# A bank table by block and group for the partial sums, and the written order of a block laid out anew

## The chip, the cores and the metric

The kernel runs on one core of one Trainium2 chip. TensorE (PE) multiplies, VectorE (DVE), ScalarE (ACT) and GpSimd (POOL) work beside it, SyncE (SP) issues transfers, and each engine takes its instructions in the order in which they are written. PSUM, where PE adds up its products, has eight banks of 128 partitions x 512 f32 values. The metric is the device time of one run in microseconds.

## The reference

Eight sequences of 4096 tokens with 192 channels go through a causal convolution with seven taps per head, softmaxed over the taps, and then through a feed-forward layer with SiLU, all in f32:

```
w = exp(weight - max); w = w / (sum(w) + 1e-09)              # 8 heads x 7 taps
out[b,s,h,:] = sum_k w[h,k] * x_pad[b, s+k, h, :]            # 24 channels a head
h = out @ w_in                                               # 192 -> 2048
g = h * (1.0 / (1.0 + np.exp(-h)))
result = g @ w_out                                           # 2048 -> 192
```

There are 32768 tokens, `w_in` is 192 x 2048 and `w_out` 2048 x 192.

## The kernel before

**Tiling.** The tokens are cut into NB = 32 blocks of 1024 (two halves of 512). Block 0 is multiplied plainly (lines 571 and 762) while the weights are rounded and combined. From block 1 on, both layers use a scheme with fewer multiplications: operands are first added and subtracted, and the products are combined by further sums.

**First layer, form R (64 rows x 128 columns of PE).** The 2048 hidden columns form five groups g = 0 to 4 and one plain chunk. A group has fifteen products `P0.g` to `P14.g` (`product`, line 611, matmul at line 625). Each has 64 rows of depth, so it sits on row group 0 or 1 (the lower or upper 64 rows). Row group 1 has r = 0, 1, 2, 4, 5, 6, 11, 14, and group 0 the others; P14.4 sits on group 0. An f32 matmul is two passes in the profile, each with its own weight load. The products of a group add up in three chains:

```
CHAINS = ((5, 2, 6, 1, 0, 14), (3, 9, 7, 4, 8), (12, 10))
```

P13 and P11 go on top of the mid-chain sums X2 and X4. After single products the chain is read while it is still open: `u` (ACT, line 674) copies the first chain to one of ten tiles in SBUF ("u tiles", handed round in a list); `X` and `a` (DVE, line 668) add the second chain to such a copy, into a bank (X) or SBUF (a); `b` (DVE) subtracts the third chain; `S` (ACT, line 686) applies SiLU. The next product of the chain waits until the reader is through with the bank, and a new chain waits for the last reader of what stood in its bank before. The plain chunk is `L.nk` (line 642; `L.0k` on group 0 alone at full width, `L.1k` on both groups at half width), with `SL` for its SiLU.

**Second layer, form C (128 rows x 32 columns).** `D i.je` (`out_slot`, line 711, matmul at line 741) is four matmuls side by side in the columns. They add into accumulator i of the block; `D5` is a quarter as wide. `t` (DVE, line 709) makes differences of the hidden values for them; `x`, `y`, `z` (ACT) and `M` (DVE) combine the accumulators, `o` transposes and `st` stores (SP).

**The next block's input.** `ld` loads (SP), `i` transposes (DVE), `ha` brings the six tokens before the block, `v.ki` is tap i of channel third k: an ACT copy into a u tile and a DMA from POOL's queue that adds it to `nat` (lines 494 and 495; for blocks up to 3 on DVE). `sp` spreads the result into the slots of `dup` (SP), and `w` (DVE) makes the combined operands in `win`. `dup` and `win` exist once.

**Order.** `PLAN` is a list of such tokens and is run once for each b from 3 to 33. A token without a sign belongs to block b, `-` to b - 1, `=` to b - 2, `+` to b + 1. So the products of a block share an iteration with the second layer of the block before. `START` is a longer list of the same kind that is run once, with b = 2, and holds blocks 0 to 2; the last C work of block 31 is in `finish`. Every instruction is pinned to this order on its engine.

**Banks.** One table serves all blocks:

```
QUEUE = (0, 4, 1, 2, 3)
CHAIN_BANKS = ((0, 1, 7, 1, 0), (2, 3, 2, 3, 2), (4, 4, 4, 4, 4))
PLAIN_BANKS = (7, 4, 3)
ACC = (7, 1, 3, 5, 6, 4, 0)
XBANK = {2: 5, 4: 6}
```

`CHAIN_BANKS[c]` has the bank of chain c for the groups in the order of `QUEUE`, `ACC` that of each accumulator. The third chain is in bank 4 for every group.

The end of R in an iteration, and the point where two late products of group 0 and block b stand between D tokens:

```
-D5.00 -S5.2 -S1.2 v.01 v.02 -D3.10 -D3.11 -S5.3 -t.20 v.23 v.24 P5.0 -P8.3 v.12 -D1.30 ...
P0.3 u1.3 b5.2 a1.2 P7.3 P12.3 S0.1 S0.0 a5.3 b1.3 P8.2 +i.1 P11.3 P14.3 S2.3 S3.3 P4.3 P10.3 D0.21 D1.20 ...
```

Of the kernel before, what the change touches and what calls it, by code (L numbers as in the profile page):

```python
# [17 lines left out]
def kernel(  # L18
# [63 lines left out]
        "-S4.3 -D1.11 -sp.0 -S1.4 -D0.11 -S5.1 -D1.01 -D0.01 -a0.2 -D1.00 -D0.10 -t.01 -t.03 "  # L82
        "-D4.01 -D4.00 ha.0 v.10 -t.10 -t.11 -S5.4 -b5.3 -D2.00 v.20 v.21 -S0.2 -t.02 -D3.01 "
        "-D2.11 -a1.3 -sp.1 -D0.31 -D2.01 -D2.10 v.00 -D3.00 -t.13 -t.12 -D5.01 v.11 v.22 -S1.3 "
        "-D4.11 -D4.10 -D5.11 -D5.00 -S5.2 -S1.2 v.01 v.02 -D3.10 -D3.11 -S5.3 -t.20 v.23 v.24 "
        "P5.0 -P8.3 v.12 -D1.30 -t.21 -D2.20 -t.23 -D4.21 -D4.20 -D5.10 -D2.21 -D0.20 -sp.2 "
        "v.03 v.04 -D5.20 -t.22 -a0.3 -D3.21 -D1.10 -w.0 -S0.3 -t.30 -t.31 -t.32 v.13 -D2.31 "
        "-D1.31 -t.33 -D5.30 -D0.00 v.05 -w.1 -w.2 -w.3 -w.4 -w.5 -D0.30 -D1.21 -D5.31 -D5.21 "
        "-x2.1 v.14 -y1.0 -D4.30 -x2.0 u5.0 -D2.30 -y2.0 -z1.0 -D3.20 -M1.0 -D4.31 -x1.0 -x2.3 "
        "-x2.2 -y0.0 +ld.1 -M2.0 -D3.31 -D3.30 -M3.0 -M4.0 P2.0 +ld.0 u4.0 P3.0 L.02 P5.4 u5.4 "  # L90
        "-x0.0 L.00 P6.0 L.12 -M5.0 u2.0 L.01 X2.0 -M7.0 P2.4 u4.4 SL.0 L.10 L.11 P9.0 SL.1 "
        "X4.0 SL.2 P1.0 u0.0 P6.4 u2.4 -M6.0 P13.0 S2.0 P5.1 u5.1 -o.3 P3.4 P7.0 P0.0 u1.0 "
        "+ld.2 P12.0 P11.0 P1.4 X2.4 P9.4 a5.0 P4.0 P13.4 b1.0 v.25 S4.0 X4.4 P10.0 a1.0 b5.0 "
        "P2.1 u0.4 P0.4 P7.4 -o.1 S2.4 a5.4 P11.4 v.26 P8.0 a0.0 u4.1 u1.4 S1.0 S4.4 P12.4 P6.1 "
        "b1.4 u2.1 P14.4 P14.0 S3.4 P3.1 X2.1 P4.4 S3.0 a1.4 P5.2 u5.2 P10.4 b5.4 P9.1 P1.1 "
        "X4.1 u0.1 -o.2 P2.2 v.06 P8.4 a0.4 P5.3 u4.2 P7.1 -st.3 a5.1 P0.1 -o.0 u5.3 u1.1 S5.0 "
        "P12.1 b1.1 P6.2 u2.2 P3.2 P4.1 a1.1 P13.1 S2.1 X2.2 P2.3 u4.3 P10.1 v.15 P1.2 u0.2 "
        "P8.1 a0.1 -st.1 b5.1 P11.1 P13.2 S4.1 S2.2 P9.2 P6.3 P14.1 P3.3 P0.2 S1.1 +i.2 P12.2 "
        "X4.2 P7.2 P11.2 u2.3 P1.3 X2.3 S3.1 P9.3 u1.2 b1.2 S4.2 P10.2 u0.3 P14.2 S3.2 v.16 "
        "-st.2 a5.2 P4.2 P13.3 X4.3 P0.3 u1.3 b5.2 a1.2 P7.3 P12.3 S0.1 S0.0 a5.3 b1.3 P8.2 "  # L100
        "+i.1 P11.3 P14.3 S2.3 S3.3 P4.3 P10.3 D0.21 D1.20 t.00 S0.4 -st.0 +i.0"
    )
    START = (
        "=dp.28 =v.20 =v.10 =dp.44 =v.00 =dp.18 =dp.6 =dp.40 =dp.7 =dp.32 =dp.23 =dp.30 =dp.13 "
        "=dp.2 =dp.20 =dp.24 =dp.15 =dp.35 =dp.14 =dp.33 =dp.11 -ld.1 =dp.37 =dp.36 =dp.25 "
        "-ld.2 =dp.27 =dp.17 -ld.0 =dp.0 =v.11 =dp.34 =v.01 =dp.26 =v.12 =dp.29 =v.21 =v.13 "
        "=dp.45 =v.22 =dp.21 =v.02 =dp.42 =v.14 =v.03 =dp.39 =v.15 =dp.3 =v.04 =dp.38 =v.16 "
        "=dp.47 =v.23 =sp.1 =v.05 =dp.1 =v.24 =dp.22 -i.1 =dp.12 =v.25 =v.06 =dp.43 =v.26 =go.2 "
        "=sp.0 =dp.19 -i.0 =dp.46 -i.2 =dp.31 -ha.0 =dp.9 =sp.2 =dp.4 =dp.41 -v.10 -v.00 -v.11 "
        "=dp.8 -v.20 -v.01 =dp.5 -v.12 =dp.16 -v.02 =w.0 =dp.10 =w.1 =cp.0 -L.01 -P5.0 -v.03 "  # L110
        "=cp.1 -L.02 -P5.4 =w.2 -u5.0 -L.10 =w.3 -u5.4 -P2.0 -P3.0 -v.13 -P2.4 -u4.0 -v.04 "
        "-P6.0 -L.00 -u4.4 -L.12 -u2.0 -L.11 -SL.0 -X2.0 -P6.4 -SL.2 =w.4 =cp.2 -P9.0 -P1.0 "
        "-u2.4 =o.0 -P13.0 -P5.1 -v.14 -u0.0 -X4.0 -P3.4 -P1.4 -S2.0 =w.5 -SL.1 -P7.0 -P11.0 "
        "-u5.1 -X2.4 -u0.4 -P12.0 -P0.0 -a5.0 -v.21 -P13.4 -P0.4 -u1.0 =o.1 -P4.0 -P9.4 -u1.4 "
        "-v.15 -S4.0 -P2.1 -P14.4 -a1.0 -b1.0 -P14.0 -P8.0 -u4.1 -X4.4 -S3.4 -P6.1 -P10.0 -v.22 "
        "-S2.4 -a0.0 -P11.4 -P7.4 -u2.1 -b5.0 -S3.0 -P5.2 -P3.1 -S4.4 -a5.4 -P1.1 -P12.4 -u5.2 "
        "-X2.1 -P4.4 -u0.1 -P9.1 -b1.4 -P2.2 -a1.4 -P10.4 -X4.1 -P5.3 -u4.2 -P8.4 =o.2 -P6.2 "
        "-b5.4 -P13.1 -u5.3 =st.2 -a0.4 -P0.1 -P7.1 -u2.2 -v.23 -S2.1 ld.1 -P2.3 -P3.2 -a5.1 "
        "-u1.1 -S0.0 -P1.2 -P12.1 -X2.2 -S0.4 -P4.1 -u4.3 -P13.2 -b1.1 ld.2 -S1.4 -P6.3 -a1.1 "
        "-u0.2 -P10.1 -v.24 -P11.1 -u2.3 -P8.1 -b5.1 -P0.2 -S4.1 -P9.2 -v.05 -S2.2 -a0.1 -P12.2 "  # L120
        "-P1.3 -u1.2 -X4.2 -S0.1 -P3.3 -P14.1 -b1.2 -u0.3 -S5.4 -P7.2 -P11.2 -X2.3 -v.16 -P10.2 "
        "-P0.3 -S4.2 -a5.2 -sp.1 -P9.3 -P14.2 -u1.3 -b5.2 -S3.1 -P13.3 -P4.2 -X4.3 -S3.2 -S1.0 "
        "i.1 -P14.3 -P12.3 =st.0 -S1.1 -a1.2 -P11.3 -P7.3 -S5.0 -v.06 -S1.2 -t.00 -D0.00 =st.1 "
        "-S3.3 -S2.3 -D1.20 -b1.3 -S5.1 ld.0 -S4.3 -t.01 -D0.01 -S5.2 -D0.21 -t.02 -D1.11 -sp.0 "
        "-a5.3 -D1.10 -v.25 -t.03 -P8.2 P5.0 +ld.1 -P4.3 -P10.3 -D1.30 -b5.3 -v.26 -D1.00 -a0.2 "
        "-sp.2 -D4.01 -t.10 -S0.2 -D5.00 -D2.01 i.0 -D4.00 -t.11 -D2.00 i.2 -D5.01 ha.0 -t.13 "
        "-D0.11 -D3.00 -a1.3 +ld.2 -D3.01 -t.12 v.10 -D4.11 -w.0 v.00 +ld.0 -D5.10 v.11 v.20 "
        "-D5.11 -D2.10 u5.0 -t.20 -D0.20 -w.1 -D3.11 -t.21 -D4.10 -w.2 -D2.11 -t.23 -P8.3 P2.0 "
        "-D0.31 -a0.3 -t.22 -D3.10 -S0.3 -S1.3 -D4.21 v.21 -S5.3 u4.0 v.01 -D4.20 -t.30 -D3.20 "
        "-D5.21 -t.31 -D2.20 -D5.20 -D2.21 -D0.10 -t.32 -D2.30 v.02 -D1.01 -t.33 -D0.30 v.03 "  # L130
        "-D1.31 v.12 -D2.31 v.04 v.22 -D1.21 v.05 -D3.30 -y1.0 -w.3 -z1.0 -D5.30 v.13 -D5.31 "
        "-D3.31 -x2.0 -M1.0 -x2.1 -D4.31 -x2.2 v.14 -x2.3 -y2.0 -M2.0 -D3.21 -y0.0 v.06 -D4.30 "
        "-x0.0 -w.4 v.23 -x1.0 P3.0 P5.4 -M3.0 L.10 u5.4 -w.5 P6.0 L.02 -M4.0 L.11 u2.0 L.00 "
        "P2.4 X2.0 P1.0 L.01 -M5.0 u4.4 v.15 L.12 u0.0 P6.4 P9.0 SL.2 SL.0 P0.0 P13.0 X4.0 SL.1 "
        "u2.4 -M7.0 P3.4 P5.1 S2.0 +i.0 P7.0 P1.4 u5.1 X2.4 P12.0 P11.0 u0.4 a5.0 u1.0 v.24 "
        "P9.4 P2.1 S4.0 b1.0 P4.0 P13.4 u4.1 X4.4 P14.0 P10.0 a1.0 P0.4 P7.4 S3.0 b5.0 v.25 "
        "P11.4 P8.0 u1.4 a5.4 S2.4 P6.1 P12.4 a0.0 P14.4 P4.4 u2.1 b1.4 v.26 P5.3 P3.1 S3.4 "
        "a1.4 S4.4 P10.4 P1.1 X2.1 P5.2 P8.4 -M6.0 u0.1 b5.4 P9.1 P0.1 u5.2 -o.1 u5.3 P13.1 "
        "P2.2 X4.1 -st.1 u1.1 +i.2 P12.1 P2.3 u4.2 a0.4 S2.1 P7.1 P6.2 b1.1 u4.3 P3.2 a5.1 P6.3 "
        "u2.2 P10.1 S5.4 X2.2 P4.1 u2.3 S0.4 P9.2 b5.1 P1.2 S0.0 a1.1 P13.2 P11.1 S1.0 -o.0 "  # L140
        "u0.2 P8.1 v.16 P1.3 S2.2 S4.1 sp.1 P0.2 P12.2 a0.1 u0.3 X4.2 S5.0 P3.3 P14.1 u1.2 +i.1 "
        "P7.2 P11.2 X2.3 -st.0 b1.2 P9.3 P0.3 S4.2 a5.2 +ha.0 P10.2 u1.3 X4.3 P4.2 S0.1 P7.3 "
        "b5.2 P14.3 S1.1 a1.2 S3.1 P12.3 P14.2 S3.3 a5.3 P13.3 -o.3 P4.3 S3.2 b1.3 -st.3 +v.10 "
        "P8.2 +v.20 a1.3 P10.3 P11.3 S5.2 t.00 S2.3 -o.2 -st.2 D0.21 D1.20"
    )
    QUEUE = (0, 4, 1, 2, 3)
    CHAIN_BANKS = ((0, 1, 7, 1, 0), (2, 3, 2, 3, 2), (4, 4, 4, 4, 4))
    PLAIN_BANKS = (7, 4, 3)
# [453 lines left out]
    ACC = (7, 1, 3, 5, 6, 4, 0)  # L602
    XBANK = {2: 5, 4: 6}

    def chain_bank(g, c):
        return banks[CHAIN_BANKS[c][QUEUE.index(g)]]

# [3 lines left out]
    def product(b, g, r, half=None):  # L611
        cols = columns(half)
        e = int(r in ON_B and (g, r) != SWAP)
        if r in RIGHT:
            rhs = rows(wins[b], e)[:, RIGHT[r], :]
        else:
            rhs = rows(dups[b], e)[:, SLOT[e][X_OF[r]], :]
        if r in (13, 11):
            to, first = banks[XBANK[2 if r == 13 else 4]], False
        else:  # L620
            c = next(c for c in range(3) if r in CHAINS[c])
            to, first = chain_bank(g, c), r == CHAINS[c][0] and (b, g, c) not in begun
            begun.add((b, g, c))
        pin(
            nc.tensor.matmul(  # L625
                to[:, cols],
                raw(g, *LEFT[e][r], e),
                rhs[:, cols],
                start=first,
                stop=True,  # L630
                skip_group_check=True,
            )
        )

    def plain(b, n, k):
# [3 lines left out]
        for e in range(2) if n else (0,):  # L639
# [3 lines left out]
                    banks[PLAIN_BANKS[n and 1 + e]][:, cols],  # L643
# [67 lines left out]
    def out_slot(b, j, i, e, half=None):  # L711
# [7 lines left out]
        if at not in accs.setdefault(b, {}):  # L719
            accs[b][at] = banks[ACC[at]]  # L720

# [389 lines left out]
```

## Time and profile before

| | us |
|---|---|
| runs (three) | 2353.54, 2353.54, 2353.39 (median 2353.54) |
| profiled execution | 2352.7, span 2351.0, granted clock 1.00 |
| PE busy | 2343.4 (100% of the span) |
| DVE, ACT, POOL busy | 1802.6, 1507.6, 528.7 |
| block 0, plain: line 571, line 762 | 41.2, 41.35 in the chain |

From about 110 us on, the same pattern returns every 72.24 us. In such a stretch (863.51 to 935.75 us) PE is busy for 72.24, DVE for 54.62, ACT for 48.54 and POOL for 15.63 us, and the DMA engines for 0.63 of the time. PE is called busy whenever any matmul is in flight, so the row says nothing of how full its two row groups or four column groups are. That has to be read from the starts of single passes, in the timeline. Times of starts are from the span's start.

### The profile page before, as it was taken

What the parts mean: (1) busy time and instruction counts of PE and PEld (TensorE: products, weight loads), DVE (VectorE), ACT (ScalarE), POOL (GpSimd) and SP (SyncE); (2) the same over time, 40 slices, a digit from 0 to 9 for tenths busy, and PEclk for the clock granted to TensorE, in tenths of its full rate; (3) what the DMA queues carried; (4) which work ended last, traced back from release to release, by engine and by line L of the source; (5) the groups of instructions that cost most, each with busy time, mean ns of one, the idle gap of its engine ahead of it and who ended that gap; (6) DMA issues with size and microseconds to landing.
All of it is one profiled execution on the core that took longest, in us unless ns stands there. A gap on an engine that the chain in (4) does not pass through costs nothing.

```text
span 2351.0 us, 45656 instructions
## 1 busy us (share of the span) xinstructions
PE 2343.4 (100%) x17630; PEld 1123.6 (48%) x17630; DVE 1802.6 (77%) x2373; ACT 1507.6 (64%) x2779; POOL 528.7 (22%) x672
## 2 busy tenths in 40 slices
PE   9999999999999999999999999999999999999998
PEld 5344554445544455444555444554445544455544
DVE  8998777787777777777777778777777777777776
ACT  5346766667666676666776666766667666677643
POOL 4920222221222211222122222122221122212200
PEclk9999999999999999999999999999999999999999
DMA  7234566665566665666656666556666566755511
GB/s 158 52 66 79 96 101 117 117 111 101 97 113 113 116 108 91 113 110 120 104 100 100 117 117 112 103 95 114 113 113 108 99 108 111 123 102 101 85 33 21
DMA packets 523833, 238.81 MB, mean 102 GB/s; under 512 B 431648, under 2 KB 436768, under 8 KB 523616
## 3 DMA queue, kind: packets, MB, share of 16 engines
q0 software_dynamic: 73024, 133.73, 33.5%
q1 hardware_dynamic: 447392, 101.78, 24.5%
q8 instruction: 138, 2.26, 0.4%
q10 hardware_dynamic: 3200, 0.39, 0.1%
q14 instruction: 79, 0.65, 0.1%
HBM read 31.46 MB, written 25.17 MB: 24 GB/s over the span
## 4 chain that ended last, share of the span: by engine, by line
PE 100%; DVE 0%; ACT 0%; issue 0%; ACTq 0%; DVEq 0%
PE ps L741 48%; PE ps L625 44%; PE ps L642 3%; PE ps L762 2%; PE ps L571 2%; PE ps L1010 1%; PE ps L418 0%; DVE cmb L158 0%; ACT u L158 0%; DVE osb L158 0%; DVE xt L460 0%; PE ps L444 0%; ACTq L944 0%; DVE zeros L158 0%; DVE xt L158 0%
## 5 line engine op out<-in xcount | busy, mean ns | idle before, releaser
L495 POOL DMA_DIRECT2D nat<-u x504 | 431.5, 953 | 1606.5 <-ACT u L494 830.7
L625 PE MATMUL ps<-win,wr 64*128 64x512 f32 x1550 | 685.8, 598 | 0.0
L741 PE MATMUL ps<-g,wo 128*32 128x512 f32 x2976 | 681.4, 594 | 0.0
L625 PE MATMUL ps<-win,ws 64*128 64x512 f32 x1550 | 629.5, 596 | 0.0
L674 ACT COPY u<-ps 128x512 f32<-128x512 f32 x775 | 452.3, 584 | 133.3 <-PE ps L625 110.7
L741 PE MATMUL ps<-t,wo 128*32 128x512 f32 (+2 forms) x4528 | 523.6, 446 | 0.0
L741 PE MATMUL ps<-t,wx 128*32 128x512 f32 x2976 | 474.7, 592 | 0.0
L686 ACT ACTIVATE g<-g 128x512 f32<-128x512 f32 x465 | 277.2, 625 | 262.6 <-DVE g L668 262.6
L625 PE MATMUL ps<-dup,wr 64*128 64x512 f32 x868 | 420.2, 598 | 0.0
L709 DVE TENSOR_TENSOR t<-g,t 128x1024 f32<-128x1024 f32 x248 | 303.0, 1222 | 134.5 <-PE ps L741 125.7
L709 DVE TENSOR_TENSOR t<-g 128x1024 f32<-128x1024 f32 x248 | 301.6, 1216 | 65.4 <-PE ps L741 65.2
L668 DVE TENSOR_TENSOR g<-u,ps 128x512 f32<-128x512 f32 x465 | 313.7, 678 | 41.4 <-PE ps L625 38.6
L494 ACT ACTIVATE u<-xt,taps 128x512 f32<-128x512 f32 x504 | 340.1, 711 | 5.1 <-DMA nat<-u 2.9
L625 PEld LDWEIGHTS ps<-win,wr 64*128 64x128 f32 x1550 | 261.6, 187 | 113.4 <-issue 61.8
L668 DVE TENSOR_TENSOR ps<-u,ps 128x512 f32<-128x512 f32 x310 | 215.0, 693 | 131.2 <-ACT u L674 60.6
L625 PEld LDWEIGHTS ps<-win,ws 64*128 64x128 f32 x1550 | 254.6, 187 | 124.2 <-issue 53.5
L686 ACT ACTIVATE g<-ps 128x512 f32<-128x512 f32 x465 | 267.4, 597 | 57.0 <-PE ps L625 56.8
L625 PE MATMUL ps<-dup,ws 64*128 64x512 f32 x682 | 291.9, 599 | 0.0
L741 PEld LDWEIGHTS ps<-t,wo 128*32 128x32 f32 x4528 | 180.3, 110 | 221.6 <-issue 192.7
L741 PE MATMUL ps<-g,wx 128*32 128x512 f32 x1488 | 251.4, 594 | 0.0
L741 PEld LDWEIGHTS ps<-t,wx 128*32 128x32 f32 x2976 | 121.2, 110 | 241.0 <-issue 240.6
L741 PEld LDWEIGHTS ps<-g,wo 128*32 128x32 f32 x2976 | 167.6, 110 | 135.3 <-issue 125.9
(92 smaller groups left out, 1883.0 us busy)
## 6 DMA issues: line engine op xcount, KB each, us to landing
nat<-u POOLq DMA_DIRECT2D x504, 256.0 KB, 4.2
dup<-nat SPq DMA_DIRECT2D x345, 128.0 KB, 2.4
nat<-in_x_dram SPq DMA_DIRECT2D x382, 64.0 KB, 4.1
out_dram<-osb SPq DMA_DIRECT2D x376, 64.0 KB, 2.1
raw<-in_moe_w_out_dram SPq DMA_DIRECT2D x8, 384.0 KB, 3.6
raw<-in_moe_w_in_dram SPq DMA_DIRECT2D x12, 192.0 KB, 4.4
ws<-wr POOLq DMA_DIRECT2D x8, 192.0 KB, 4.7
raw<-in_moe_w_in_dram SPq DMA_DIRECT2D x6, 128.0 KB, 3.0
```

Source lines behind the costliest of these rows:

```text
L494: pin(nc.scalar.activation(z, src, AF.Copy, scale=tap))
L495: pin(nc.gpsimd.dma_start(out=dst, in_=z, accum_op=ALU.add))
L571: nc.tensor.matmul(hs[a, n, e], rows(wr[j], e)[:, a, k, :], rows(d, e)[:, n, k, :], start=k == 0, stop=k == NK - 1,)
L625: nc.tensor.matmul(to[:, cols], raw(g, *LEFT[e][r], e), rhs[:, cols], start=first, stop=True, skip_group_check=True,)
L642: nc.tensor.matmul(banks[PLAIN_BANKS[n and 1 + e]][:, cols], rows(wr[j] if own == e else ws[j], e)[:, a, k, :], rows(dups[b], e)[:, SLOT[e ...
L668: pin(nc.vector.tensor_tensor(out_, u, v, op=op))
L674: pin(nc.scalar.copy(us[b, g, o][:, cols], t1[:, cols]))
L686: pin(nc.scalar.activation(h, src, AF.Silu))
L709: pin(nc.vector.tensor_tensor(t[i // 2][:, i % 2, :], u, v, op=ALU.subtract))
L741: nc.tensor.matmul(accs[b][at][SQ * q : SQ * q + SQ, to], lhs[:, e, SQ * k : SQ * k + SQ], rhs[:, e, ts(q, TB // 4) if i == 5 else to], st ...
L762: nc.tensor.matmul(banks[DOWN_BANKS[k]][R * n : R * n + R, :], wo[j][:, a, e, R * k : R * k + R], gs[b, j, a][:, n, e, :], start=j == 0 an ...
L1010: nc.tensor.matmul(by_pe[k][n], rows(diag, n)[:, k, i, :], rows(xts[0], n)[:, k, i : i + TB], start=i == 0, stop=i == K - 1,)
```

## The change

Every table of banks gets one entry for each chain, mid-chain sum, plain sum and accumulator, by group, and three versions: for block 1, block 2, and all later ones. The lookups take the block. `PLAN` and `START` are written anew. They hold the same tokens apart from some signs. Nothing that is computed changes.

```diff
-    CHAIN_BANKS = ((0, 1, 7, 1, 0), (2, 3, 2, 3, 2), (4, 4, 4, 4, 4))
-    PLAIN_BANKS = (7, 4, 3)
+    CHAIN_BANKS = (
+        ((1, 0, 1, 3, 6), (5, 7, 5, 4, 2), (3, 6, 6, 1, 4)),
+        ((0, 0, 3, 7, 4), (3, 1, 6, 2, 6), (1, 2, 5, 1, 5)),
+        ((0, 7, 0, 6, 2), (4, 1, 3, 2, 5), (6, 4, 1, 5, 3)),
+    )
+    XBANKS = (
+        ((7, 3, 2, 2, 4), (7, 5, 0, 7, 4)),
+        ((5, 4, 4, 0, 5), (7, 5, 5, 4, 7)),
+        ((3, 4, 5, 4, 3), (1, 2, 5, 7, 6)),
+    )
+    PLAIN_BANKS = (
+        (0, 2, 3),
+        (2, 2, 1),
+        (6, 5, 7),
+    )
+    ACC = (
+        (3, 2, 5, 6, 7, 1, 0),
+        (4, 6, 3, 5, 1, 7, 0),
+        (4, 7, 5, 1, 3, 6, 0),
+    )
...
-    ACC = (7, 1, 3, 5, 6, 4, 0)
-    XBANK = {2: 5, 4: 6}
-
-    def chain_bank(g, c):
-        return banks[CHAIN_BANKS[c][QUEUE.index(g)]]
+
+    def of_block(table, b):
+        return table[min(b, len(table)) - 1]
+
+    def chain_bank(b, g, c):
+        return banks[of_block(CHAIN_BANKS, b)[c][g]]
+
+    def x_bank(b, g, o):
+        return banks[of_block(XBANKS, b)[o // 2 - 1][g]]
+
+    def plain_bank(b, i):
+        return banks[of_block(PLAIN_BANKS, b)[i]]
...
-            accs[b][at] = banks[ACC[at]]
+            accs[b][at] = banks[of_block(ACC, b)[at]]
...
-    DOWN_BANKS = (4, 5, 6)
+    DOWN_BANKS = (7, 4, 2)
```

The new `PLAN`, without the stretch of D tokens in its middle (where a line of dots stands for lines left out):

```
P5.0 -a1.3 -P10.2 -a0.2 -P10.3 -b5.3 -P8.3 -S4.3 -sp.0 -D0.31 -S0.1 -S1.0 -D1.10 v.20
-S3.3 -D1.30 -S1.4 -D1.21 -D0.00 -t.00 -t.01 -D2.00 -D2.01 =st.1 v.11 -t.03 -D4.01
-S1.1 -t.10 -D4.00 -D5.00 v.00 v.01 -D0.10 -sp.2 -t.11 -D2.10 -D1.01 v.12 -b5.2 v.02
...
-D3.01 -D1.11 -D5.11 -w.1 -D5.01 +ld.2 -D1.31 v.14 v.04 -D0.11 -D3.11 -D1.20 -a0.3
v.15 u5.0 -S1.2 -S0.2 -t.20 -D0.20 -t.21 -D2.21 -t.22 -S0.3 -D2.20 -w.2 v.22 -S1.3
+ld.1 -S5.3 -t.23 -D4.20 -D4.21 -D5.21 -D5.20 -D3.20 v.05 -t.30 -t.31 -D1.00 -t.33
-D2.31 -D5.31 -D5.30 -x2.2 -x2.0 v.23 -D0.30 -D0.21 -D0.01 -y0.0 v.06 -t.32 -z1.0 v.24
+ld.0 -D2.30 -w.3 -y1.0 -D3.21 -x2.3 -x2.1 -M1.0 -w.5 -D3.30 v.25 -D3.31 -x0.0 -D4.30
-D4.31 -y2.0 P2.0 -x1.0 -w.4 -M2.0 u4.0 -M6.0 P5.4 u5.4 P3.0 L.00 -M3.0 -M4.0 L.11
v.16 P6.0 -M5.0 -M7.0 L.02 u2.0 P2.4 u4.4 X2.0 v.26 L.12 -o.3 L.10 SL.1 SL.2 +i.0 P1.0
u0.0 L.01 SL.0 P6.4 u2.4 P13.0 -o.0 S2.0 -o.2 P9.0 P5.1 P3.4 X4.0 P0.0 u1.0 X2.4 P12.0
P11.0 P7.0 S4.0 b1.0 a5.0 P1.4 P14.0 -st.2 P13.4 u5.1 +i.2 P10.0 u0.4 S3.0 b5.0 P4.0
...
b1.4 P14.4 P11.4 P10.4 u2.1 a0.0 S3.4 S4.4 a5.4 P2.2 u4.2 P4.4 X2.1 P13.1 S2.1 b5.4
P9.1 a1.4 +i.1 P1.1 X4.1 P6.2 P3.2 u0.1 P8.4 a0.4 u2.2 X2.2 P5.3 P0.1 u5.3 P7.1 +ha.0
P11.1 S0.0 P12.1 P2.3 P9.2 a5.1 P4.1 P13.2 u1.1 b1.1 P10.1 P1.2 a1.1 +v.10 S4.1 u4.3
sp.1 S2.2 X4.2 b5.1 u0.2 P6.3 u2.3 P3.3 S5.1 X2.3 S0.4 P14.1 P8.1 a0.1 P11.2 S4.2 P7.2
P0.2 S3.1 a5.2 u1.2 P9.3 X4.3 P12.2 P1.3 P4.2 S5.0 a1.2 u0.3 b1.2 P13.3 S2.3 P7.3 a5.3
P14.2 S3.2 P0.3 u1.3 P12.3 S5.4 -st.0 P11.3 P8.2 b1.3 P4.3 P14.3
```

In `PLAN` the last line is followed by the first one of the next iteration.

## The prediction

> **What bounds the kernel now.** I read the page first, then the chain in order of time, then the timeline of TensorE (PE) and of its weight loads (PEld) at the places where the chain changes line.
>
> ```profile
> PE 2343.4 (100%) x17630; PEld 1123.6 (48%) x17630; DVE 1802.6 (77%) x2373; ACT 1507.6 (64%) x2779; POOL 528.7 (22%) x672
> PE 100%; DVE 0%; ACT 0%; issue 0%; ACTq 0%; DVEq 0%
> ```
>
> PE sets the end; no other engine holds a share of the chain. A gain or a loss is therefore time in which PE's row or column groups do nothing, and that does not show as idle PE. The chain of one block:
>
> ```profile
> 904.25 29.82 PE ps L625 x135
> 934.08 18.82 PE ps L741 x192
> 952.90 1.06 PE ps L625 x4
> 953.96 17.54 PE ps L741 x192
> 971.49 1.48 PE ps L625 x5
> ...
> 976.50 29.82 PE ps L625 x135
> ```
>
> The same line returns after 72.25 us. A block is a stretch of L625 and L642 (products, call it R) and L741 (D tokens, call it C), and it changes form four times: R, C 18.82, a detour of two products (P5.0, P8.3) of 1.06, C 17.54, R. Now the timeline at the detour:
>
> ```profile
> 879.61 1.04 PE L741 MATMUL ps<-t,wo 128*32 128x512 f32 x8
> 880.59 0.69 PE L625 MATMUL ps<-dup,wr 64*128 64x512 f32 x1
> 880.59 0.69 PE L625 MATMUL ps<-win,wr 64*128 64x512 f32 x1
> 881.12 0.59 PE L625 MATMUL ps<-dup,wr 64*128 64x512 f32 x1
> 881.12 0.59 PE L625 MATMUL ps<-win,wr 64*128 64x512 f32 x1
> 881.64 0.63 PE L741 MATMUL ps<-g,wx 128*32 128x512 f32 x3
> ```
>
> Each product is two passes. On one row group passes start 0.429 us apart, so a product takes 0.858 there, and the other group (other 64 rows) runs beside it. After a change of form the first pass takes 0.53 (its weights are not loaded ahead), and the last 0.52. A trip C to R and back costs 0.11 (last D token, 0.972 for 0.858) + 0.10 + 0.10 + 0.025 = 0.34 us. Last, the end of R, PE and then PEld:
>
> ```profile
> 930.47 0.59 PE L625 MATMUL ps<-win,ws 64*128 64x512 f32 x1
> 930.66 1.02 PE L625 MATMUL ps<-win,wr 64*128 64x512 f32 x2
> 931.10 0.69 PE L625 MATMUL ps<-dup,wr 64*128 64x512 f32 x1
> 931.52 0.59 PE L625 MATMUL ps<-win,wr 64*128 64x512 f32 x1
> 931.63 0.59 PE L625 MATMUL ps<-dup,wr 64*128 64x512 f32 x1
> 931.95 0.59 PE L625 MATMUL ps<-win,wr 64*128 64x512 f32 x1
> ```
> ```profile
> 930.66 0.19 PEld L625 LDWEIGHTS ps<-win,wr 64*128 64x128 f32 x1 [0.24 <-issue]
> 931.09 0.19 PEld L625 LDWEIGHTS ps<-win,wr 64*128 64x128 f32 x1 [0.24 <-issue]
> 931.09 0.29 PEld L625 LDWEIGHTS ps<-dup,wr 64*128 64x128 f32 x2
> 931.52 0.19 PEld L625 LDWEIGHTS ps<-win,wr 64*128 64x128 f32 x1
> ```
>
> The order there is P0.3 (row group 1), P7.3, P12.3, P8.2 (all 0), P11.3 (1). Group 1 is free at 930.47 + 0.43 = 930.90, but P11.3 (the dup,wr row) starts at 931.10, right after P12.3 has started and the weights of its second pass have been issued. It then runs ahead of P8.2 (931.95), which stands before it. So PE passes over waiting work of the other group, but not over any amount. I counted this over all PE and PEld rows, at the moment its own group came free: of 487 loads with five loads and passes of the other group waiting ahead of them, 280 left within 0.06 us (readers of banks held the rest); of 34 with seven to nine ahead (P11.3 in 30 blocks) none did, and the least late was 0.51 late. Call this the limit of five.
>
> **The parts.** A block holds 40 full D tokens at 0.858 and 8 D5 at 0.218: 36.07 us. On each row group it holds 39 products or L.0 and three half-width L.1 at 0.43: 34.76. Together 70.83, so 1.41 of the 72.24 is loss: two trips, 0.68, and waits inside R of 0.71 (0.27 round P10.4 and P9.1, where P9.1 waits for X2.1 to read bank 2 and for DVE, which restarts it unloaded; 0.44 from P7.3 to P10.3, where b1.3 reads bank 4, which all groups' third chain shares). The work itself is unchanged: the same 9,331 tokens, 17,144 matmuls, and on ACT, DVE, POOL and SP the same instructions in another order.
>
> *One trip less.* P5.0 and P8.3 join P10.2 and P10.3 at the end of R: -0.34.
>
> *Bank waits.* The third chain gets several banks, so P10.3 no longer waits last, and X2.1 reads well before P9.1. I went through the new order product by product, setting each reader (u 0.585, X 0.69, a 0.68, b 0.69; starts 0.60 apart when queued, 0.59 from a pass's start to its end, 0.04 to 0.05 each way between engines) against the row group's next product. The old -0.71 goes. One wait comes: a0.4, X2.2 and a5.1 stand in a row on DVE behind P8.4, and P4.1 needs a5.1. From P8.4's second pass this takes 0.59 + 0.04 + 0.60 + 0.61 + 0.68 + 0.05 = 2.57. Row group 1 has 3.00 until P4.1 if both groups run level, but group 0 is 0.51 late here (next part), leaving 2.49: a wait of 0.08 to 0.11 and a restart of 0.10. Bounds: 0 (level) and 0.6 (P9.2, P13.1, P6.2, P11.0, P4.0 have 0.16 to 0.24 to spare by the same reckoning; two of them late with a restart each). I take +0.22, nearest to the P9.1 stop.
>
> *The limit of five in the new order.* It stands at two places. P2.4, L.12, L.10, P1.0, L.01: L.01 must pass L.10 and P1.0 of group 1, so it waits 0.43 and starts unloaded: 0.51 late, but group 0 has that to spare. Then the end: P4.3, P14.3, P5.0 (all group 1), P10.2, P10.3, P8.3 (all group 0). P10.2 cannot pass until P14.3 has started; then it starts unloaded (0.11) and three products follow on group 0, 2.57, while group 1 has only P14.3 and P5.0 left, 1.72. R ends 0.97 later than level groups would. Bounds: 0 (no limit) and 2.15 (no passing). The P11.3 rows are the same situation: +0.97. This is the term that eats the gain.
>
> The Trainium skill, in TensorE: Matmul & The Clock Gate, section "Step-by-step: what each phase is for", says that only weight loads are pulled ahead and matmuls stay in program order. By that rule P10.2 would start with P5.0's second pass, 1.18 later than in my sum; the trace speaks against it, since P11.3 starts 0.85 before P8.2.
>
> *Moved conv steps.* v.11 to v.05 lie in C as before (12 pairs of an ACT copy, 0.71, and a POOL DMA, 4.2 to landing), v.23, v.06, v.24, v.25, v.16, v.26 now at the end of C and early in R, not spread over R. ACT has 48.5 busy of 72.2 and waits in C; cost 0 while the u tiles come free (rival below). *Moved on SP:* sp.1 and ha.0's two DMAs go to the end of R, the load order becomes 2, 1, 0, and st.1 goes one iteration later, behind sp.0, which waits for P13.3 and P14.3. Some 37 issues of about 0.55, 20 us of 72; sp.1 should land 4 us before P5.0. Cost 0. *START:* 153.3 us now; by the same prices 150.85, so 2.5 of waits. It has as many changes of form as before. Bounds -2.5 to +2.5; with the bank waits shorter I take -1.0. *End:* one trip less, -0.3.
>
> **Sum.** Per block -0.34 - 0.71 + 0.22 + 0.97 = +0.14; by stretches 36.07 + 34.76 + 0.34 + 0.97 + 0.22 = 72.36, +0.12. Times 29 blocks: +3.5; START and end -1.3: +2.2. The profiled execution took 2352.7 (span 2351.0), so 2354.9; the median of the runs stands 0.8 above it: 2355.7, say 2355. Within 0.2% (4.7 us) is about what a measurement can tell from no change.
>
> **Rivals.**
> - *The limit does not bind* (faster). Then both 0.97 and 0.22 go, -1.05 x 29 - 1.3 = -32: 2322. Against it: those 34 cases. The Trainium skill, TensorEngine Tiling (Array Packing), "Key Properties", has the tiles operate independently, which would give this; the 931.10 row disagrees. 0.11.
> - *The limit binds, R's other waits go, START gains more:* -0.11 x 29 and -4: about 2345. 0.14.
> - *Small DVE waits* (slower): two of the products with 0.16 to 0.24 to spare stop, 0.2 each: +11, 2366. For it: DVE is busy some 31 of R's 36 us. 0.22.
> - *The u tiles run out* (slower). u1.0 reuses the tile that v.25's DMA reads. v.23, v.24, v.25 follow one another on one nat slice; at 4.2 each, v.25 is in 2.2 before u1.0, and P14.0 has 0.9 more. It decides from about 5.2 each (landings of up to 6.8 occur); at 5.5 it is 0.8 a block, +23: 2377. Against it: single ones land in 3.3. 0.06.
> - *No passing at all:* +1.18 x 29 = +34: 2389. Refuted by the P11.3 rows, unless those are special. 0.03.
>
> **Numbers.** My forecast, no change, 0.44, with a range of its own of 2349 to 2358. Faster 0.11 + 0.14 = 0.25; slower 0.22 + 0.06 + 0.03 = 0.31. Leaving out 2322, 2377 and 2389 (0.20), the range is 2342 to 2370.
>
> **What would show it.** One R and one C piece per block in the chain, no 1.06 piece. At R's end a first weight load of P10.2 (dup,ws) right after P14.3's first pass, and R's end with only group 0 at work for about 0.9 us. L.01 about half a microsecond late. P9.1 and P10.3 without a wait on DVE, P4.1 with one. A period of 72.1 to 72.6. I am wrong if P10.2 starts beside P4.3 (period near 71.2), or if ACT waits for POOL at u1.0.

## The result and the profile after

| | before | after |
|---|---|---|
| median of the runs, us | 2353.54 | 2368.28 (2367.17 to 2368.87, four runs) |
| ratio | | 1.0062, 95% interval 1.0045 to 1.008 |
| profiled execution (span) | 2352.7 (2351.0) | 2367.17 (2365.1) |
| period of a block from block 4 on | 72.24 | 72.55 |
| START, first pass to first pass of the next iteration | 153.34 | 156.24 |

The changed kernel is 0.62% slower: 14.7 us by the medians, 14.5 between the profiled executions. The forecast was no change, 2355. Two stretches hold the loss. The blocks take 0.31 us more each, 29 times, 9.0 us. START takes 2.9 more although two products and two D tokens, 2.57 us of PE's work, have moved out of it to the last iterations: 5.5 in all, which is also what the blocks' 9.0 leave of the 14.5.

The page of the changed kernel, busy times and the chain's shares:

```profile
PE 2352.3 (99%) x17630; PEld 1156.1 (49%) x17630; DVE 1797.8 (76%) x2373; ACT 1503.1 (64%) x2779; POOL 530.3 (22%) x672
PE 97%; DVE 2%; issue 0%; SPq 0%; ACT 0%; DMA 0%; DVEq 0%; ACTq 0%
```

PE is idle for 12.8 us of the span (7.6 before), and DVE now holds 2% of the chain: that is START. The chain of one block, in order of time (start, length, what):

```profile
871.76 36.22 PE ps L765 x384
907.98 1.48 PE ps L649 x5
...
944.31 5.70 PE ps L765 x49
```

C (L765) is one piece and no 1.06 us piece of products stands in it: the second trip is gone. R now lasts from 907.98 to 944.31. Its end, PE and then PEld:

```profile
940.44 0.59 PE L649 MATMUL ps<-win,wr 64*128 64x512 f32 x1
...
941.46 1.13 PE L649 MATMUL ps<-dup,ws 64*128 64x512 f32 x4
942.32 0.59 PE L649 MATMUL ps<-dup,wr 64*128 64x512 f32 x1
...
942.75 0.59 PE L649 MATMUL ps<-dup,wr 64*128 64x512 f32 x1
...
943.29 1.02 PE L649 MATMUL ps<-win,wr 64*128 64x512 f32 x2
944.24 1.07 PE L765 MATMUL ps<-g,wo 128*32 128x512 f32 x8
```
```profile
941.46 0.30 PEld L649 LDWEIGHTS ps<-dup,ws 64*128 64x128 f32 x3 [0.24 <-issue]
```

P8.2 (win,wr, group 0) starts its second pass at 940.44, so group 0 is free at 940.87. P10.2 (dup,ws, like P14.3) starts only at 941.47, beside P14.3's first pass: its weights are among the three loads of 941.46. P5.0 (dup,wr, group 1) has its last pass at 942.75 and leaves group 1 free at 943.18. Group 0 goes on with P10.3 and P8.3 to 944.15. That is the 0.97 us with one group only, to the hundredth.

The stop at P4.1, DVE and then PEld:

```profile
928.92 0.69 DVE L692 TENSOR_TENSOR g<-u,ps 128x512 f32<-128x512 f32 x1 [0.94 <-PE ps L649]
929.72 0.70 DVE L692 TENSOR_TENSOR ps<-u,ps 128x512 f32<-128x512 f32 x1
930.32 0.68 DVE L692 TENSOR_TENSOR g<-u,ps 128x512 f32<-128x512 f32 x1
```
```profile
931.06 0.18 PEld L649 LDWEIGHTS ps<-win,ws 64*128 64x128 f32 x1 [0.29 <-DVE g L692]
```

These are a0.4, X2.2 and a5.1, and P4.1's first load. Its first pass starts with it, 0.29 late and unloaded, and so its second pass comes another 0.10 late. From a0.4 to X2.2 it takes 0.80, from X2.2 to a5.1 0.60.

By the terms of the prediction the block now adds up: 36.07 (C) + 34.76 (R) + 0.34 (one trip) + 0.97 (end of R) + 0.40 (P4.1) = 72.54, measured 72.55.

START. First DVE and PE of the changed kernel, then DVE of the kernel before, then busy time by stretch of the changed kernel (window, length, PE, PEld, DVE, ACT, POOL with counts, PEclk, DMA share, GB/s):

```profile
98.23 0.69 DVE L550 TENSOR_TENSOR win<-dup 128x512 f32<-128x512 f32 x1 [5.55 <-DMA dup<-nat]
...
103.18 7.84 DVE L516 SCALAR_TENSOR_TENSOR nat<-xt,taps,nat 128x512 f32<-128x512 f32 x9
...
112.33 0.68 DVE L692 TENSOR_TENSOR ps<-u,ps 128x512 f32<-128x512 f32 x1
```
```profile
113.07 0.69 PE L649 MATMUL ps<-dup,wr 64*128 64x512 f32 x1 [4.62 <-DVE ps L692]
...
114.31 1.06 PE L649 MATMUL ps<-win,ws 64*128 64x512 f32 x1
...
115.16 1.06 PE L649 MATMUL ps<-win,ws 64*128 64x512 f32 x1
```
```profile
95.18 3.35 DVE L499 SCALAR_TENSOR_TENSOR nat<-xt,taps,nat 128x512 f32<-128x512 f32 x4 [2.80 <-ACT nat L491]
...
106.74 0.69 DVE L668 TENSOR_TENSOR ps<-u,ps 128x512 f32<-128x512 f32 x1 [2.15 <-ACT u L674]
```
```profile
113.00:114.00 1.00, 0.93 (x4) 0.71 (x6) 1.00 (x3) 0.00 (x0) 0.86 (x3) 0.87 0.00 0
114.00:117.50 3.50, 3.50 (x11) 1.71 (x9) 1.85 (x3) 1.66 (x3) 3.27 (x7) 0.55 0.48 75
```

In the new order twelve taps (`v` of block 2, on DVE for blocks up to 3; nine of them in the row of 103.18) and a transpose stand between the first `w` and X2.0 (112.33). P13.0 waits for X2.0, and PE stands still for 4.62 us. In the kernel before, four taps ran ahead of the first `w` (95.18), three more between it and X2.0, and ahead of X2.0 (106.74) DVE was waiting for ACT. Then something new: after the pause the granted clock is 0.87 and 0.55 in these two rows (it is 0.50 from 113.74 to 117.15 and 1.00 around that), passes start 0.85 apart instead of 0.43 (114.31 to 115.16). Each row group loses 1.70 us to it, half of 3.41.

### The profile page after: what moved, and what is told of

It reads as the page before. It is cut to its first block, busy times and chain, and to the rows that moved or that the text cites. A ratio compares the mean times of both kernels' runs of the same rounds, so it can differ in the third digit from the quotient of the medians.

```text
span 2365.1 us, 45608 instructions
## 1 busy us (share of the span) xinstructions
PE 2352.3 (99%) x17630; PEld 1156.1 (49%) x17630; DVE 1797.8 (76%) x2373; ACT 1503.1 (64%) x2779; POOL 530.3 (22%) x672
## 4 chain that ended last, share of the span: by engine, by line
PE 97%; DVE 2%; issue 0%; SPq 0%; ACT 0%; DMA 0%; DVEq 0%; ACTq 0%
PE ps L765 47%; PE ps L649 45%; PE ps L666 2%; PE ps L588 2%; DVE nat L516 1%; PE ps L1034 1%; DVE two L175 0%; DVE g L692 0%; PE ps L435 0%; DVE mh L175 0%; SPq L533 0%; DVE xt L477 0%; DVE t L733 0%; DMA dup<-nat 0%; DVE ps L692 0%
## 5 line engine op out<-in xcount | busy, mean ns | idle before, releaser
L765 PE MATMUL ps<-g,wo 128*32 128x512 f32 x2976 | 681.1, 593 | 0.0
L649 PE MATMUL ps<-win,wr 64*128 64x512 f32 x1550 | 648.2, 594 | 0.0
L649 PE MATMUL ps<-win,ws 64*128 64x512 f32 x1550 | 617.7, 595 | 0.2 <-DVE ps L692 0.2
L698 ACT COPY u<-ps 128x512 f32<-128x512 f32 x775 | 444.0, 587 | 135.3 <-PE ps L649 115.5
L765 PE MATMUL ps<-t,wo 128*32 128x512 f32 (+1 forms) x4528 | 523.5, 446 | 0.0
L765 PE MATMUL ps<-t,wx 128*32 128x512 f32 x2976 | 475.1, 592 | 0.6 <-DVE t L733 0.6
L649 PE MATMUL ps<-dup,wr 64*128 64x512 f32 x868 | 442.6, 591 | 4.6 <-DVE ps L692 4.6
L649 PEld LDWEIGHTS ps<-win,ws 64*128 64x128 f32 x1550 | 264.6, 187 | 99.0 <-issue 34.3
L765 PEld LDWEIGHTS ps<-t,wo 128*32 128x32 f32 x4528 | 180.1, 110 | 220.3 <-issue 209.7
L649 PE MATMUL ps<-dup,ws 64*128 64x512 f32 x682 | 273.2, 594 | 0.0
L823 ACT COPY yx<-ps 32x128 f32<-32x128 f32 x120 | 30.8, 257 | 364.5 <-PE ps L765 363.1
L765 PEld LDWEIGHTS ps<-t,wx 128*32 128x32 f32 x2976 | 121.7, 110 | 278.4 <-issue 250.6
L765 PE MATMUL ps<-g,wx 128*32 128x512 f32 x1488 | 245.3, 592 | 0.0
```

The costliest lines, as they stand in the source:

```text
L649: nc.tensor.matmul(to[:, cols], raw(g, *LEFT[e][r], e), rhs[:, cols], start=first, stop=True, skip_group_check=True,)
L698: pin(nc.scalar.copy(us[b, g, o][:, cols], t1[:, cols]))
L765: nc.tensor.matmul(accs[b][at][SQ * q : SQ * q + SQ, to], lhs[:, e, SQ * k : SQ * k + SQ], rhs[:, e, ts(q, TB // 4) if i == 5 else to], st ...
L823: nc.scalar.copy(to[:, ts(q, TB // 4)], acc[5][SQ * q : SQ * q + SQ, 0 : TB // 4])
```

## The experiments

In the diffs below, lines of the written order are cut to the tokens that matter, and a line of dots stands for lines left out.

### The end of R, taking turns

```diff
- S5.4 -st.0 P11.3 P8.2 b1.3 P4.3 P14.3
+ S5.4 -st.0 P11.3 P8.2 b1.3 P4.3 P10.2 P14.3 a1.3 P10.3 +P5.0 P8.3
```

A token whose work is done is passed over, so the tokens P5.0, -P10.2, -P10.3 and -P8.3 at the head of the next iteration do nothing any more.

> The end of R is written as P11.3, P8.2, P4.3, P10.2, P14.3, P10.3, P5.0, P8.3, so that the row groups take turns and no weight load has more than five loads and passes of the other group waiting ahead of it. Theory (the limit of five holds P10.2 back in the changed kernel): the 0.97 us a block in which only group 0 works goes, less what the two groups stay apart by the wait at P4.1 (0.3 us): 0.64 to 0.97 a block, 19 to 28 us in all, so 2340 to 2349 us. Rival (P10.2 is held by b1.2, a1.2 or its bank, not by the order on PE): under 0.1 us a block, 2365 to 2370 us.

Measured: 2349.18 us (2348.27 to 2349.73), 0.9981 of the kernel before (0.9972 to 0.999), 19.1 us less than the changed kernel and at the edge of what was expected; the period is 71.85, 0.70 less. The end of R, PE:

```profile
934.93 0.59 PE L649 MATMUL ps<-win,wr 64*128 64x512 f32 x1
...
935.36 0.59 PE L649 MATMUL ps<-dup,ws 64*128 64x512 f32 x1
```

P8.2's second pass starts at 934.93 and P10.2 at 935.36, 0.43 later: on time. The same products on the same banks, with the same DVE and ACT steps, lose 0.70 less once P10.2 stands in another place on PE. So it is the order on PE that holds P10.2. What is left of the 0.97 is group 0 being behind by 0.27.

### Two products ahead, not three

```diff
- S5.4 -st.0 P11.3 P8.2 b1.3 P4.3 P14.3
+ S5.4 -st.0 P11.3 P8.2 b1.3 P4.3 P14.3 P10.2 a1.3 +P5.0 P10.3 P8.3
```

> The changed kernel with the end of R written as P11.3, P8.2, P4.3, P14.3, P10.2, P5.0, P10.3, P8.3: two products of row group 1 stand between P8.2 and P10.2, not three as in the changed kernel and not one as in the alternating order. Theory (five loads and passes may wait ahead: of P4.3 and P14.3 at most five are left when group 0 comes free): P10.2 leaves as in the alternating order, 2348 to 2350 us. Rival (only one product, four loads and passes, can be passed, or none): P10.2 waits for P4.3 to be through, 0.4 us or more a block above that, 2360 to 2368 us.

Measured: 2349.23 us, period 71.85, the same as with turns. PEld of this kernel, with P10.2's two loads and P14.3's first:

```profile
936.00 0.61 PEld L649 LDWEIGHTS ps<-dup,ws 64*128 64x128 f32 x3
```

Group 0 can take P10.2's weights once P8.2's second pass has started, at 935.84. Seven loads and passes wait ahead of that load then; in all 29 steady blocks it leaves 0.16 us later, when five are left, and the pass is on time. In the changed kernel eleven wait ahead of it, and it leaves 1.02 later (940.44 to 941.46). Counted over the rows of the changed kernel, for the first loads of products: of 249 loads with five ahead 210 left within 0.06 us, of 156 with seven ahead none before 0.11, and of 58 with eleven (P10.2 and L.01) none before 0.63. The limit of five holds here, as read from the trace of before.

### L.01 alone

```diff
- X2.0 v.26 L.12 -o.3 L.10 SL.1 SL.2 +i.0 P1.0 u0.0 L.01 SL.0 P6.4
+ X2.0 v.26 L.12 -o.3 L.01 L.10 SL.1 SL.2 +i.0 P1.0 u0.0 SL.0 P6.4
```

> Only L.01 moves, in front of L.10, in every block from 3 on. Theory (L.01's half microsecond is hidden by itself, but it makes row group 0 late, and that is why a5.1 and with it P4.1 come late): L.01 starts on time, P4.1's wait of 0.29 + 0.10 us goes, the end of R stays as it is: 0.2 to 0.4 us a block, 6 to 12 us, so 2356 to 2362 us. Rival (the row a0.4, X2.2, a5.1 on DVE is late by itself, or the end of R gives it back): 2367 to 2370 us.

Measured: 2357.71 us (1.0017, 1.0009 to 1.0026), 10.6 less; period 72.15, 0.40 less. P4.1's load still waits for a5.1 in the rows, but both of its passes are on time, and P10.2 is as late as in the changed kernel (0.63 us, 0.60 there). So the half microsecond of L.01 is indeed hidden where it stands, and comes out at P4.1, 20 us further on.

### The detour put back

```diff
- P5.0 -a1.3 -P10.2 -a0.2 -P10.3 -b5.3 -P8.3 -S4.3
+ -a1.3 -P10.2 -a0.2 -P10.3 -b5.3 -S4.3
...
- -D2.00 -D2.01 =st.1 v.11
+ -D2.00 -D2.01 P5.0 -P8.3 =st.1 v.11
```

> The changed kernel with the detour of the old PLAN put back: P5.0 and P8.3 stand between D2.01 and =st.1 among the D tokens again (b5.3 behind P10.3), the rest is untouched. Theory (P5.0 at the end of R is what holds P10.2 back, so the trip saved costs more than it brings): without P5.0 only P4.3 and P14.3 wait ahead of P10.2, it leaves some 0.6 earlier, and the trip costs 0.34: 0.28 a block less, 8 us, so 2359 to 2361 us. Rival (the end of R stays as it is and the trip is paid): 0.34 a block more, 10 us, so 2378 us.

Measured: 2359.37 us (1.0025, 1.0015 to 1.0035), 8.9 less; period 72.18, 0.37 less, a little more than the 0.28 expected. The chain has its detour again:

```profile
874.78 1.06 PE ps L649 x4
...
906.04 1.48 PE ps L649 x5
...
940.81 4.41 PE ps L765 x37
```

R takes 34.77 us (906.04 to 940.81) for 36.33: 0.86 for the product that each group has less, and 0.70 besides. The part of the change that saves a trip costs time in this order: it puts P5.0 ahead of P10.2 as a third product of group 1.

### One trip by itself

The diff is against the kernel of the last experiment below (old start, turns at the end of R, L.01 moved).

```diff
- P5.0 -a1.3 -P10.2 -a0.2 -P10.3 -b5.3 -P8.3 -S4.3
+ -a1.3 -P10.2 -a0.2 -P10.3 -b5.3 -S4.3
...
- -D2.00 -D2.01 =st.1 v.11
+ -D2.00 -D2.01 P5.0 -P8.3 =st.1 v.11
...
- P4.3 P10.2 P14.3 a1.3 P10.3 +P5.0 P8.3
+ P4.3 P10.2 P14.3 a1.3 P10.3
```

> The price of one trip by itself: the kernel with the old start, the alternating end of R and L.01 in front of L.10 (2329.0 us), with P5.0 and P8.3 taken out of the end of R and put between D2.01 and =st.1. Here no weight load has more than five ahead of it with or without them. Theory (a trip from D tokens to products and back costs 0.34 us wherever it stands): 0.29 to 0.34 a block, 8 to 10 us more, 2337 to 2339 us. Rival (the sum of the prediction had the trip right only by chance, it is hidden or costs more where it parts the D tokens elsewhere): under 3 or over 14 us more.

Measured: 2339.84 us against 2329.0, 10.8 more, a little above what was expected; the period grows from 71.43 to 71.76, 0.33. The expectation is not quite right on the loads: in both kernels three loads of a block have seven ahead of them. That costs the same in both, 0.10 us at P13.0, so the difference of the periods is the trip's: it costs what the rows of before gave.

### The start undone

```diff
     START = (
-        "=dp.0 =v.00 -ld.2 =v.01 =v.02 =v.20 =v.21 =v.03 =v.04 =v.05 =v.06 =dp.1 =dp.2 =dp.3 "
+        "=dp.28 =v.20 =v.10 =dp.44 =v.00 =dp.18 =dp.6 =dp.40 =dp.7 =dp.32 =dp.23 =dp.30 =dp.13 "
...
     CHAIN_BANKS = (
-        ((1, 0, 1, 3, 6), (5, 7, 5, 4, 2), (3, 6, 6, 1, 4)),
-        ((0, 0, 3, 7, 4), (3, 1, 6, 2, 6), (1, 2, 5, 1, 5)),
+        ((0, 7, 1, 0, 1), (2, 2, 3, 2, 3), (4, 4, 4, 4, 4)),
+        ((0, 7, 1, 0, 1), (2, 2, 3, 2, 3), (4, 4, 4, 4, 4)),
```

> The start alone is undone: the written order of blocks 0 to 2 and the banks of blocks 1 and 2 are those of the kernel before (two accumulators of block 2 exchanged, S5.1 of block 2 written there), PLAN and the banks from block 3 on are the new ones. Theory (some 5.5 of the 14.7 us are lost in the start, 9 in the steady blocks): 2362 to 2364 us. Rival (the start only takes over or hands on work, and the blocks hold all of the loss): 2367 to 2370 us.

Measured: 2361.06 us (1.0032, 1.0019 to 1.0044), 7.2 less. START and the iteration behind it take 223.0 instead of 229.0, 6.0 less. The period of a block is unchanged, 72.55. The start is a loss by itself. It is a little more than the 5.5 that were read from the stretches (2362 to 2364 us were expected); the runs of the changed kernel lie 1.7 us apart, so no more is to be had from the difference.

### What bounds the start

Three experiments on START. The first fills DVE's wait for the DMA:

```diff
- -ha.0 =go.2 -v.20 =dp.37 =dp.38 =sp.2 =w.0 =dp.39
+ -ha.0 =go.2 -v.20 -v.10 -v.00 -v.11 -v.21 -v.01 -v.12 =dp.37 =dp.38 =sp.2 =w.0 =dp.39
...
- -P5.0 -v.00 =dp.43 =dp.44 -v.10 -v.11 -v.12 =w.1
+ -P5.0 =dp.43 =dp.44 =w.1
...
- =cp.0 -v.01 -v.13 =dp.46 =dp.47 =cp.2 -v.21 -v.22
+ =cp.0 -v.13 =dp.46 =dp.47 =cp.2 -v.22
```

> In the new start four taps that DVE makes for block 2 (v.11, v.21, v.01, v.12) and the ACT steps v.10 and v.00 before them are written ahead of w.0 of block 1, where DVE waits 5.55 us for a DMA. Theory (DVE is the bound of the start from there on; 95 of its steps have to be through before the last t of block 1, 84 in the kernel before): the wait of PE for X2.0 falls from 4.8 to about 1.4 us, the 1.7 us at half the clock behind it go, 5 us in all, about 2363 us. Rival (PE's wait is for something else, or DVE only loses the time at another place): 2367 to 2370 us.

Measured: 2366.67 us (2364.29 to 2367.74), 1.6 less than the changed kernel, whose runs reach down to 2367.17: a miss. DVE of this kernel:

```profile
97.94 3.36 DVE L516 SCALAR_TENSOR_TENSOR nat<-xt,taps,nat 128x512 f32<-128x512 f32 x4 [4.53 <-ACT nat L508]
101.22 0.94 DVE L550 TENSOR_TENSOR win<-dup 128x512 f32<-128x512 f32 x1
```

The room was not there. The taps need an ACT step on `xt`, and that waits 5.50 us for the DMA that brings the six tokens before the block. It runs from 96.57 on (95.82 in the changed kernel, 94.4 in the kernel before; all of this run is 0.66 us later than the changed kernel's from block 0's line 786 on). So the taps push the first `w` from 98.23 to 101.22, 2.3 us without that shift, and PE's wait only falls to 3.7 us.

The second moves X2.0 ahead of the last taps, and leaves nothing out:

```diff
- -L.00 -v.02 -v.03 =cp.1 -v.23
+ -L.00 -v.02 =cp.1
...
- -P3.0 -L.10 -v.04 -v.05 ld.0 -P6.0 -u2.0 =o.2 -P2.4 -u4.4 -L.12 -L.11 -SL.2 -SL.1
- -v.24 ld.1 -X2.0 =o.1
+ -P3.0 -L.10 ld.0 -P6.0 -u2.0 -P2.4 -u4.4 -L.12 -L.11 -SL.2 -SL.1
+ ld.1 -X2.0 -v.03 -v.23 -v.04 -v.05 =o.2 -v.24 =o.1
```

> In the new start X2.0 of block 1 is written ahead of the five taps v.03, v.23, v.04, v.05, v.24 and a transpose that stand before it on DVE. Nothing is left out. Theory (DVE is the bound of the whole start from the first w on): PE's wait at 108.5 goes and with it the 1.7 us at half the clock, but the time that the taps take comes back as later waits: 1.5 to 2.5 us less, 2366 to 2367 us. Rival (only the order is at fault, DVE has room further on): 4.8 + 1.7 = 6.5 us less, 2362 us.

Measured: 2367.79 us, 0.5 less than the changed kernel, within its runs. PE's wait on DVE in 97 to 218 us (total, times, longest):

```profile
PE ps L649 <- DVE ps L692: 3.9, 1, 3.9
```

The wait is still there, 3.9 us, now further on, for an X behind the same taps; and as it is again one long pause, the slow clock comes with it too (0.58 in 114 to 117.5 us, 0.74 in 117.5 to 125). Here it lasts 6.83 us, twice as long as in the changed kernel's trace, so the two times can't be compared to better than a microsecond or so. The expectation had the time coming back in small pieces, without the slow clock. The order of X2.0 isn't the main cause.

The third leaves five taps out:

```diff
- -L.00 -v.02 -v.03 =cp.1 -v.23
+ -L.00 -v.02 =cp.1
...
- -P3.0 -L.10 -v.04 -v.05 ld.0 -P6.0
+ -P3.0 -L.10 ld.0 -P6.0
...
- -v.24 ld.1 -X2.0 =o.1
+ ld.1 -X2.0 =o.1
```

> In the new start the same five taps (v.03, v.23, v.04, v.05, v.24 of block 2) are left out, so the convolution of block 2 lacks them; all else is as in the changed kernel. Theory (DVE is the bound of the start): five times 0.855, 4.3 us, and the 1.7 us at half the clock go and stay away: 6 us less, 2362 to 2363 us. Rival (DVE is not the bound; the start waits for transfers or for the order on PE): under 2 us less, 2366 to 2368 us.

Measured: 2361.19 us, 7.1 less, a little more than expected. START takes 150.1 instead of 156.2. The same wait of PE (this kernel's lines are lower by one):

```profile
PE ps L648 <- DVE ps L691: 0.4, 1, 0.4
```

4.3 us of DVE's work taken away give 6.1 us in START: the 4.3, and the 1.7 at half the clock. DVE bounds this stretch. The written orders say why it does so more than before. From the first `w` of block 1 to the last `t` of block 1, both counted, DVE has 84 steps in the old START and 97 in the new one: 18 taps of block 2 for 14, 10 taps of block 3 for 4, 12 `w` for 9, the rest alike. (The 95 of the expectation end at t.33, which is not the last `t` in the new START.)

### All three mended

Old START with its banks, turns at the end of R, L.01 in front of L.10.

> Old start, the alternating end of R and L.01 in front of L.10, all three together. Theory (three separate losses: the limit of five at the end of R, P4.1's wait, DVE in the start): 2361.1 for the old start, less 19.1 for the end of R, less 10.6 for L.01: 2331 to 2333 us, period 71.4 to 71.5 us. Rival (the gains overlap, since both the end of R and P4.1 are about which row group is behind): 2337 to 2342 us.

Measured: 2329.0 us (2328.86 to 2329.89), 0.9897 of the kernel before (0.9884 to 0.9911), 39.3 less than the changed kernel and 2 below what was expected; the period is 71.43.

In its chain C is the same 36.22 as in the changed kernel, and R takes 35.20 (892.51 to 927.71) for 36.33. PE is busy for 2320.1 us of a span of 2328.1. The sum of the three single gains was 36.9; they don't overlap. By the periods the two gains in the block are 0.70 and 0.40 alone and 1.12 together. This kernel beats both: the new layout of a block, with one trip and its own banks, is worth 1% once its three flaws are out.

## Why the prediction was right and wrong

The time lies inside the range and outside the case that was called likeliest. That the range held it is in part luck: its upper end came from a rival with more stops in every block, and START, which took half of the error, had been bounded at 2.5. The sum gave 2354.9 for the profiled execution, which took 2367.2. Of the 12.3 us between them 6.5 are START and 5.5 the wait at P4.1 (29 times 0.19).

- *One trip less, -0.34.* Right: no detour in the chain, and 0.33 by the experiment on the trip alone.
- *Old bank waits, -0.71.* Right: in the steady blocks neither P9.1 nor P10.3 waits, and with the other two flaws out the period is 71.43, 0.26 above what the work and one trip come to (71.17). How much of this the banks give and how much the order was not tried apart.
- *Limit of five, +0.97.* Right in place, size and cause, and this term decides whether a block gains. That it can be avoided in the same layout was not asked.
- *L.01 late but hidden.* Right, and the coupling to P4.1 that was named is the one that the experiment shows.
- *P4.1, +0.22.* The mechanism was right, the size not: 0.40. The mis-sized part is the step of 0.60 from a0.4 to X2.2, which took 0.80. Two things end just before X2.2: a0.4, at 929.61, and u2.2 on ACT, at 929.55. X2.2 needs both, since it reads u2.2 and writes bank 5, the bank that a0.4 reads (the new table gives it to X2 of group 2 and to the second chain of group 4). The trace has a0.4's end as the last release. Which of the two would have to go was not tried.
- *START, -1.0 (bounds -2.5 to +2.5).* Wrong, +5.5, beyond both bounds. The step that failed is "by the same prices 150.85, so 2.5 of waits": it laid out PE's work, and took the waits from the old START. In START DVE has the taps of blocks 2 and 3 to do, and the count of DVE's steps ahead of each product was in the two lists. The bounds left out the slow clock too, since no stretch of before that was read shows one.
- *Moved conv steps, 0.* Right in the blocks, wrong in START, where the same steps are DVE's.
- *End, -0.3.* Not to be told apart from the 2.57 us that moved there.

Of the rivals, "the limit does not bind" and "no passing at all" are refuted by the two experiments on the end of R. "The u tiles run out" did not occur. "Small DVE waits" named nearly the right time, 2366, but mostly by another way: there is the larger stop at P4.1 and a restart of 0.10 at P9.2, none at P13.1, P6.2, P11.0 or P4.0, and the rest of the loss is START.

The Trainium skill, TensorE: Matmul & The Clock Gate, section "Step-by-step: what each phase is for", has matmuls in program order. The rows of the changed kernel disagree as those of before did: P5.0 is written ahead of P10.2 and starts at 942.32, 0.85 after it.

## What to carry to other kernels

When a written order is laid out anew, go through it once for each engine and not only for the one that bounds the whole: a stretch like the start can have another bound, and there a count of the steps ahead of each result tells it. Let work for the two row groups take turns, and look at how many loads and passes of one group stand ahead of the other's next one: a merge that saves a trip can lose more than the trip. A hidden delay is not free, as it shifts one group against the other and shortens the slack of every wait behind it.

## What the runs showed that was not expected

A pause of PE of 4.6 us costs more than itself. Passes were slow (granted clock 0.50, 0.85 us apart for 0.43) from 0.67 us after the pause for 3.41 us, 1.70 us on each row group; with the wait moved (3.9 us) it came again, for 6.83 us. It also differs from run to run. Five kernels here have the same START (the changed one and those with turns, with two ahead, with L.01 moved and with the detour): the slow stretch lasts 3.41 us in three of their traces and 6.83 us in two, and START takes 156.2 to 157.7 us. So a difference of a microsecond between the times of two of them says nothing, and the periods are the better measure of a block. The Trainium skill, TensorE: Matmul & The Clock Gate, section "Part 1: The HAM clock gate (the "warmup" mystery)", says that the array falls to half its rate after an idle window of about 3.4 us and rises again after a busy one, and that the window runs freely; by that rule some 3.4 us of half speed cost 1.7, and the traces agree in the length, 3.41 us and twice that.
